# Sliding-window attention with a gated MLP: the values of batches 2 to 7 as 64x64 quarters, in one block with the next scores

## The chip, the cores and the metric

The kernel runs on one core of a Trainium2 chip. The metric is the device time of one execution in microseconds, the median of three runs. The engines are TensorE (matmuls; its weight loads are listed apart), VectorE, ScalarE, GpSimd, and the SP queue, which here only issues DMAs. Each works through its own instructions in the order in which the program lists them, and waits on semaphores for the others.

## The reference

```python
# attention: batch 8, heads 8, sequence 576, head_dim 64; window 128
scores = scale * np.matmul(q, k.transpose(0, 1, 3, 2))
rel = pos[:, None] - pos[None, :]
bias = slopes[:, None, None] * (-np.abs(rel))[None, :, :]
mask = (rel >= 0) & (rel < window)
scores = np.where(mask, scores + bias[None], -1000000000.0)
attn = softmax(scores)
x = np.matmul(attn, v)                 # (8, 8, 576, 64) -> 4608 tokens of 512
# MLP: d_model 512, d_ff 2048
h = x @ w_in
g = h * np.clip(h + 3.0, 0.0, 6.0) / 6.0
out = g @ w_out
```

A query sees itself and the 127 keys before it. With query blocks of 128 that is the block of its own (below the diagonal) and the one before (above the diagonal). With halves of 64 it is three key halves: its own, the one before, which lies wholly inside the window, and the one before that.

## The kernel before

The two stages run interleaved. Attention works on pairs of heads: `g` runs from 0 to 31, four pairs to a batch (`NP` = 4), and `e` is the head within the pair. The MLP works on nine tiles of 512 tokens. Its work is cut into units: an up (`moe_up`, 4 matmuls of 512 columns into an `hps` bank, then a relu on ScalarE and a product on VectorE that also frees the bank) and a quarter of a down (`moe_down`, 4 matmuls into `ops`). The order of ups and downs is a hand-written string (L564), and `fill(n)` issues the next n units; it stops early where an up needs tokens whose attention isn't marked `done`.

Batches 0 and 1 have code of their own (`first_batch`, `second_batch`). Batches 2 to 7 run in `segment` (L718), one turn for each `g` from 8 to 32. A turn issues the scores of `g`, then between units its exponentials and masks, and the values of `g - 1`. Every engine's order is the program's order (`manual_schedule`), so the place of a line in `segment` is its place in each queue.

- Scores (`scores`, L344): keys on the partitions of the result. From g = 9 on they are 20 matmuls on 64x64 quarters of the array (row half by head, column half by key half), up to 192 columns each, into the two tiles `sce` (two banks each, pool `ps_sc`). These two tiles are kept through all of the segment. At g = 8 `scores_whole` writes them with 128-row results, so that no part is left unwritten.
- Exponentials and masks: `exp_diag` and `exp_off` (L385, L410) turn `sce` into `pd` (own block), `po` (block before) and `p4buf` (the last 64 queries), bf16; the ALiBi bias is the activation's bias, by partition (`bias_d`, `bias_o`). GpSimd clears what lies outside the window by `affine_select` (L406, L415, L421).
- Values (`values`, L445): the probabilities are the weights, and the values with a column of ones (`vbuf`, 65 columns) are streamed. 18 matmuls on the whole array, in two parts of 10 and 8, each part into the one bank of `ps_av`. VectorE divides by the column of sums (L452, L453) into `avs`.
- `back` (L472): an SP transpose DMA brings `avs` to `xT`, the MLP's input; for g = 10 and 11 TensorE and ScalarE do.
- `stage_next` (L591): the loads of a later batch on the SP queue (`load_tokens`), GpSimd's casts into `tbuf` and `vbuf`, and the SP transposes from `tbuf` into `qTb` and `kTb` (`xbar`). There is one `tbuf`, so the cast of the keys waits until the queries' transpose has read it.
- `double` (L237): for g = 8 to 11, TensorE transposes of keys and queries of batches 2 and 3 through a PSUM bank.

PSUM pools before: `ps_sc` 2 tiles of two banks, `ps_av` 1 bank, `ps_h` 2 banks (ups, transposes), `ps_o` 1 bank (downs). A tile of a pool takes the bank of the tile allocated as many allocations earlier as the pool has buffers, and waits until that one's last reader is done.

## Time and profile before

| | |
|---|---|
| median of three runs | 322.15 us (321.69 to 322.75) |
| the profiled execution's span | 319.2 us |
| granted TensorE clock, mean | 0.999 |
| VectorE, ScalarE, GpSimd busy | 173.1, 195.7, 141.2 us |
| DMA | 51.90 MB, mean 163 GB/s |

The span runs from the first to the last instruction of the program in one profiled execution. Busy time is summed by engine. A timeline row gives the start, the length from the first start to the last end of merged instructions, engine, line, operation, result and operands, and a count. A group row of the page gives the busy time, the mean length of one, and the engine's idle time ahead of it. A row of one line's or tile's instructions gives the shortest, median and longest in ns, then the first and the last start in us. A matmul's length includes its way through the array, and the next starts before it ends. ScalarE's and VectorE's lengths also overlap a little with the next.

### The profile page before, as it was taken

Reading aid. Unit: us, or ns where it says so; the run is one execution under the profiler, and the core shown is the slowest. Engines: PE = TensorE matmul, PEld = TensorE weight load, DVE = VectorE, ACT = ScalarE, POOL = GpSimd, SP = SyncE. Lnnn points to the kernel's source line nnn. Section 1 sums busy time; section 2 is a strip of 40 time slices with the busy share of each in tenths; the row PEclk is TensorE's granted clock in tenths of the full one; section 3 lists DMA queues with packets and bytes.
Section 4 is the critical chain, followed back from the end, with each engine's and each line's share of the span. In section 5 each row is a group of like instructions: output and inputs, shape, how many; then the busy total and the mean of one; then the engine's idle time right before and its main releaser. Section 6 shows DMA issues by size and latency. Waiting matters only on the chain.

```text
span 319.2 us, 7124 instructions
## 1 busy us (share of the span) xinstructions
PE 310.1 (97%) x2775; PEld 164.9 (52%) x2775; DVE 173.1 (54%) x338; ACT 195.7 (61%) x334; POOL 141.2 (44%) x249
## 2 busy tenths in 40 slices
PE   7879999999999999999999999999999999999996
PEld 5565465455545454445677654444444444444443
DVE  6667675554355655655565556555656455455510
ACT  4748976877767776676676667666764344244401
POOL 8464493684496477266744673663331000000000
PEclk9999999999999999999999999999999999999999
DMA  7999999999999999998999999962212110000112
GB/s 281 199 323 225 256 260 195 249 231 194 215 252 157 239 208 211 205 222 194 207 205 211 209 190 196 225 93 68 38 39 88 53 36 33 33 33 35 66 56 75
DMA packets 131425, 51.90 MB, mean 163 GB/s; under 512 B 118976, under 2 KB 123328, under 8 KB 131392
## 3 DMA queue, kind: packets, MB, share of 16 engines
q1 hardware_dynamic: 126160, 45.36, 68.0%
q0 software_dynamic: 4224, 4.19, 8.2%
q10 hardware_dynamic: 1008, 1.90, 1.6%
q8 instruction: 21, 0.34, 0.5%
q14 instruction: 12, 0.10, 0.1%
HBM read 36.70 MB, written 9.44 MB: 145 GB/s over the span
## 4 chain that ended last, share of the span: by engine, by line
PE 86%; DMA 5%; ACT 4%; POOL 2%; DVE 2%; issue 1%; POOLq 0%
PE ops L552 38%; PE hps L502 36%; DMA w_in_sb<-in_moe_w_in_dram 3%; PE sce L365 3%; PE av L442 2%; PE av L434 2%; DMA ldbuf<-in_k_dram 2%; ACT r L521 2%; PE ops L533 1%; ACT kTb L245 1%; ACT gbuf L399 1%; PE tp L243 1%; DVE gbuf L522 0%; ACT gbuf L377 0%; PE tb L483 0%
## 5 line engine op out<-in xcount | busy, mean ns | idle before, releaser
L522 DVE SCALAR_TENSOR_TENSOR gbuf<-r,hps 128x512 bf16<-128x512 f32 x144 | 98.7, 688 | 101.0 <-ACT r L521 99.8
L521 ACT ACTIVATE r<-hps,bias 128x512 f32<-128x512 f32 x144 | 98.9, 689 | 86.8 <-PE hps L502 86.6
L502 PE MATMUL hps<-xT,w_in_sb 128*128 128x512 bf16 (+1 forms) x640 | 144.9, 358 | 0.6 <-ACT xT L489 0.3
L552 PE MATMUL ops<-w_out_sb,gbuf 128*128 128x512 bf16 x560 | 137.8, 379 | 0.0
L502 PEld LDWEIGHTS <-w_in_sb 128*128 128x128 bf16 x640 | 59.3, 98 | 55.0 <-issue 0.8
L552 PEld LDWEIGHTS <-gbuf 128*128 128x128 bf16 x560 | 51.9, 98 | 56.3
L415 POOL TENSOR_SCALAR_AFFINE_SELECT po<-po 128x512 bf16<-128x512 bf16 x48 | 30.3, 636 | 32.5 <-ACT po L413 32.4
L406 POOL TENSOR_SCALAR_AFFINE_SELECT pd<-pd 128x512 bf16<-128x512 bf16 x48 | 29.8, 634 | 33.5 <-ACT pd L389 33.5
L389 ACT ACTIVATE pd<-sce,bias_d 128x512 bf16<-128x512 f32 x48 | 31.7, 684 | 5.4 <-PE sce L373 2.7
L561 DVE COPY osb<-ops 128x512 f32<-128x512 f32 x33 | 22.7, 688 | 20.0 <-PE ops L552 17.5
L195 POOL CAST tbuf<-ldbuf 128x512 bf16<-128x512 f32 (+1 forms) x45 | 25.6, 614 | 16.8 <-issue 9.3
L413 ACT ACTIVATE po<-sce,bias_o 128x512 bf16<-128x512 f32 x48 | 33.0, 687 | 0.0
L453 DVE TENSOR_TENSOR avs<-av,rc 128x384 bf16<-128x384 f32 (+1 forms) x48 | 23.6, 491 | 1.6
L442 PEld LDWEIGHTS <-pd 128*128 128x128 bf16 x192 | 14.3, 97 | 8.3 <-issue 0.5
L434 PE MATMUL av<-vbuf,po 128*128 128x65 bf16 x192 | 18.0, 193 | 0.0
L442 PE MATMUL av<-vbuf,pd 128*128 128x65 bf16 x192 | 17.3, 193 | 0.3 <-ACT kTb L245 0.3
L434 PEld LDWEIGHTS <-po 128*128 128x128 bf16 x192 | 14.3, 98 | 2.9 <-DVE avs L453 0.5
L188 POOL CAST vbuf<-ldbuf 128x1024 bf16<-128x1024 f32 x14 | 14.2, 1043 | 3.5 <-DMA ldbuf<-in_v_dram 3.5
L418 ACT ACTIVATE p4buf<-sce,bias_d 128x64 bf16<-128x64 f32 x48 | 15.5, 323 | 0.0
L228 POOL CAST pr<-ldbuf 128x576 bf16<-128x576 f32 x20 | 12.9, 670 | 5.1 <-DMA ldbuf<-in_k_dram 3.1
L365 PE MATMUL sce<-qTb,kTb 64*64 64x192 bf16 (+1 forms) x368 | 11.9, 245 | 0.0
L365 PEld LDWEIGHTS <-kTb 64*64 64x64 bf16 x368 | 7.1, 106 | 8.6 <-issue 8.5
(104 smaller groups left out, 208.4 us busy)
## 6 DMA issues: line engine op xcount, KB each, us to landing
out_dram<-osb SPq DMA_DIRECT2D x33, 256.0 KB, 2.5
ldbuf<-in_v_dram SPq DMA_DIRECT2D x32, 256.0 KB, 5.2
ldbuf<-in_q_dram SPq DMA_DIRECT2D x20, 256.0 KB, 5.3
ldbuf<-in_k_dram SPq DMA_DIRECT2D x16, 256.0 KB, 4.4
ldbuf<-in_q_dram SPq DMA_DIRECT2D x12, 288.0 KB, 7.0
ldbuf<-in_k_dram SPq DMA_DIRECT2D x12, 288.0 KB, 6.3
w_in_sb<-in_moe_w_in_dram POOLq DMA_DIRECT2D x4, 512.0 KB, 9.2
w_out_sb<-in_moe_w_out_dram POOLq DMA_DIRECT2D x4, 512.0 KB, 10.3
```

What stands on the lines that cost most here:

```text
L195: nc.gpsimd.tensor_copy(out=tbuf[:m, :, j, :], in_=s[:m, j, :, :].rearrange("p (i e) d -> p i (e d)", e=2))
L365: nc.tensor.matmul(sce[e][lo:lo + 64, j, :, :].rearrange("p s c -> p (s c)")[:, ds(lo, n)], lhsT=kT[r, j, lo:lo + 64], rhs=qT[r, ds(128 * ...
L389: nc.scalar.activation(out=pd[:, e, :, :], in_=st["sce"][e][:, :, 0, :], func=ACT.Exp, bias=bias_d[:, h:h + 1], scale=scale)
L406: nc.gpsimd.affine_select(out=pd[:, e, :, :], in_=pd[:, e, :, :], pattern=[[0, 4], [1, 128]], channel_multiplier=-1, base=0, compare_op=AL ...
L413: nc.scalar.activation(out=po[:, e, :, :], in_=sc[:, :, 1, :], func=ACT.Exp, bias=bias_o[:, h:h + 1], scale=scale)
L415: nc.gpsimd.affine_select(out=po[:, e, :, :], in_=po[:, e, :, :], pattern=[[0, 4], [-1, 128]], channel_multiplier=1, base=-1, compare_op=A ...
L434: nc.tensor.matmul(out_av, lhsT=po[:, e, qt % 4 if full(g) else qt - 1, :], rhs=vb[:, qt - 1, h, :], start=True, stop=False)
L442: nc.tensor.matmul(out_av, lhsT=d, rhs=vb[:, qt, h, :], start=(qt == 0), stop=True)
L502: nc.tensor.matmul(hps[:, lo:hi], lhsT=w_in_sb[:, ks, ts(ms, 128)], rhs=xT[:, ks, ds(src, hi - lo)], start=(ks == 0), stop=(ks == n_ks - 1))
L521: nc.scalar.activation(out=r6, in_=hps, func=ACT.Relu, bias=bias3[:, 0:1], scale=1.0 / 6.0)
L522: nc.vector.scalar_tensor_tensor(out=gts[nt][:, ms, :], in0=r6, scalar=1.0, in1=hps, op0=ALU.min, op1=ALU.mult)
L552: nc.tensor.matmul(ops[nt, sub], lhsT=gts[nt][:, ms, ts(sub, 128)], rhs=w_out_sb[:, ms, :], start=(ms == 0), stop=(ms == n_ms - 1))
```

## The change

From batch 2 on, the scores and the values both go by quarters. A query half meets its own key half (`back` = 0), the one before (1) and the one before that (2). The scores of each `back` stand together in the score tile (`SLOT`, `COUNT`, `place`), so each is one activation for each head, six for a pair in all: 320, 256 and 256 columns. The mask for `back` = 0 and 2 is one `affine_select` for each partition half over both heads; `back` = 1 needs none. A quarter's result lies on the partition half given by the parity of the query half and by the head, so half of the value matmuls need the values on the other partition half: `vswap` is a copy of `vbuf` with its halves swapped, made by VectorE in four parts a batch.

In a turn, the values of `g - 1` now follow the scores of `g` at once; only the values of g = 8 come in the middle of turn 9, behind the four parts of `vswap` for batch 2. `back` is issued after the third unit. The exponentials come in the order 0, 2, 1, the last after the sixth unit. There are seven units in turns 9 to 16 and eight in the others; before, seven in turns 9 to 11 and 13 to 15, and eight in the others, as far as `fill` doesn't stop early. The pool `ps_av` goes, and `ps_h` has three banks: values take two of them at a time, and `double`, the warm-up and some of the first ups move to it. At g = 8 four matmuls of 512 columns write all of the score tiles ahead of the quarters. The biases by partition half (`bias_s`) are made ahead of the segment, and `bias_o` and `p4buf` go.

```diff
-    ps_av = ctx.enter_context(tc.tile_pool(name="ps_av", bufs=1, space=bass.MemoryType.PSUM))
-    ps_h = ctx.enter_context(tc.tile_pool(name="ps_h", bufs=2, space=bass.MemoryType.PSUM))
+    ps_h = ctx.enter_context(tc.tile_pool(name="ps_h", bufs=3, space=bass.MemoryType.PSUM))
...
+    def half_biases():
+        nc.vector.tensor_scalar(out=rel_f[64:128, :], in0=rel_f[64:128, :], scalar1=-64.0,
+                                scalar2=0.0, op0=ALU.add, op1=ALU.add)
+        for back in range(3):
+            for h in range(H):
+                nc.vector.tensor_scalar(out=bias_s[:, back, h:h + 1], in0=rel_f,
+                                        scalar1=-32.0 - 64.0 * back, scalar2=slopes[h],
+                                        op0=ALU.add, op1=ALU.mult)
...
+    COUNT = (5, 4, 4)
+    SLOT = (0, 9, 5)
+
+    def place(back, qh):
+        k, b = divmod(qh, 2)
+        return (k + 1) % NQ if back == 0 else k - (back + 1 - b) // 2
...
         if g == 2 * NP:
...
+            st["sc"] = [ps_sc.tile([128, 16 * 64], FP32, tag="sc", name="sc") for _ in range(2)]
+            for bank in range(2):
                 for e in range(2):
                     r = slice(e * D, (e + 1) * D)
...
+                    nc.tensor.matmul(st["sc"][e][:, ts(bank, 512)], lhsT=kT[r, 0:128],
+                                     rhs=qT[r, 0:512], start=True, stop=True)
+        for m in range(9):
+            both = m < 6
+            for back in (0, 1) if both else (0, 2, 1):
+                if m + back > 8:
+                    continue
+                qh = m + back
+                for e in range(2):
+                    r = slice(e * D, (e + 1) * D)
+                    c0 = 64 * (qh % 2 ^ e)
+                    at = SLOT[back] + place(back, qh)
+                    o = st["sc"][e][c0:c0 + 64, :].rearrange("p (j c) -> p j c", c=64)
+                    x = qT.rearrange("p (j c) -> p j c", c=64)
+                    if both and back == 0:
+                        o, x = o[:, at:at + 5:4, :], x[r, m:m + 3:2, :]
+                    else:
+                        o, x = o[:, at, :], x[r, qh, :]
+                    nc.tensor.matmul(o, lhsT=kT[r, ts(m, 64)], rhs=x, start=True, stop=True)
...
+    def exp_back(g, back, e):
+        h, p, n = 2 * (g % NP) + e, st[g, "p"][back], COUNT[back]
+        nc.scalar.activation(out=p[:, e, :, :].rearrange("p j c -> p (j c)"),
+                             in_=st["sc"][e][:, ds(64 * SLOT[back], 64 * n)], func=ACT.Exp,
+                             bias=bias_s[:, back, h:h + 1], scale=scale)
+        if e == 0 or back == 1:
+            return
+        for r in range(2):
+            half = p[ds(64 * r, 64), :, :, :].rearrange("p e j c -> p (e j) c")
+            sign, base = (1, 0) if back == 0 else (-1, -1)
+            nc.gpsimd.affine_select(out=half, in_=half, pattern=[[0, 2 * n], [sign, 64]],
+                                    channel_multiplier=-sign, base=base,
                                     compare_op=ALU.is_ge, fill=0.0)
...
+    def values(g):
+        b, hp = divmod(g, NP)
+        av = [ps_h.tile([128, NT], FP32, tag="h", name="av") for _ in range(2)]
+        steps = [[(qh, back) for qh in range(half, 9, 2) for back in range(3) if qh >= back]
+                 for half in range(2)]
+        steps[1].append((9, 0))
+        for i in range(len(steps[0])):
+            for half in range(2):
+                if i >= len(steps[half]):
+                    continue
+                qh, back = steps[half][i]
+                k, qh = qh // 2, min(qh, 7 + (half == 0))
+                at = place(back, qh)
+                for e in range(2):
+                    r = slice(64 * (half ^ e), 64 * (half ^ e) + 64)
+                    v = (vbuf if back % 2 == e else vswap)[b % 2]
+                    nc.tensor.matmul(av[e][ts(half, 64), ds(k * W, W)],
+                                     lhsT=st[g, "p"][back][r, e, at, :],
+                                     rhs=v[r, (qh - back) // 2, 2 * hp + e, :],
+                                     start=(back == 0),
+                                     stop=(back == min(2, qh) or k == 4 and half == 1))
+        avs = st[g, "avs"] = small.tile([128, NQ, 2, D], BF16, tag="avs", name="avs")
+        rc = small.tile([128, 2, NQ, 1], FP32, tag="rcw", name="rcw")
+        for e in range(2):
+            a = av[e][:, 0:NQ * W].rearrange("p (j c) -> p j c", j=NQ)
+            nc.vector.reciprocal(rc[:, e, :, :], a[:, :, D:W])
+            nc.vector.tensor_tensor(out=avs[:, :, e, :], in0=a[:, :, 0:D],
+                                    in1=rc[:, e, :, :].to_broadcast([128, NQ, D]), op=ALU.mult)
+
+    def swap_v(b, part):
+        lo, j0, j1 = ((0, 0, 3), (64, 0, 2), (0, 3, 5), (64, 2, 4))[part]
+        nc.vector.tensor_copy(
+            out=vswap[b % 2][ds(64 - lo, 64), j0:j1, :, :].rearrange("p j h c -> p (j h c)"),
+            in_=vbuf[b % 2][ds(lo, 64), j0:j1, :, :].rearrange("p j h c -> p (j h c)"))
...
+    UP_BANKS = {5: "o", 11: "o"}
...
+    FILLS = {g: 7 for g in range(9, 17)}
+
+    def segment(lo, hi):
         for g in range(lo, hi + 1):
+            b, hp = divmod(g, NP)
+            swaps = list(range(4)) if hp == 0 and b < B and g > lo else []
             if by_xbar(g - 2):
                 done[0] = g - 1
+            if lo < g < hi:
                 scores(g)
+            if g > lo + 1:
+                values(g - 1)
+            if g == 3 * NP:
+                cast_tokens(3, "v")
             turn = {2 * NP: (2, 1, "k"), 2 * NP + 1: (2, 1, "q"),
                     2 * NP + 2: (3, 0, "k"), 2 * NP + 3: (3, 1, "k")}.get(g)
             if turn:
+                double(*turn, 0, "h", A)
+            elif g < hi:
+                exp_back(g, 0, 0)
+            fill(1)
             if turn:
+                double(*turn, 1, *(("h", V) if turn[0] == 2 else ("h", A)))
+                exp_back(g, 0, 0)
+            fill(1)
             if g < hi:
+                exp_back(g, 0, 1)
+            fill(1)
+            if g > lo + 1:
+                back(g - 1)
+                if not by_xbar(g - 1):
+                    done[0] = g
             if g < hi:
+                exp_back(g, 2, 0)
+            for part in range(4):
+                if g == lo + 1:
+                    swap_v(2, part)
+            fill(1)
             if g < hi:
+                exp_back(g, 2, 1)
+            if swaps:
+                swap_v(b, swaps.pop(0))
+            if g == lo + 1:
+                values(g - 1)
+                back(g - 1)
+            fill(1)
             if g < hi:
+                exp_back(g, 1, 0)
+            if swaps:
+                swap_v(b, swaps.pop(0))
+            fill(1)
             if g < hi:
+                exp_back(g, 1, 1)
                 stage_next(g)
+            if swaps:
+                swap_v(b, swaps.pop(0))
             fill(1)
+            if swaps:
+                swap_v(b, swaps.pop(0))
+            fill(FILLS.get(g, 8) - 7)
```

125 lines of the change are left out of this document (14 added, 111 removed).

## The prediction

> **What bounds the kernel now.** I read the page first (busy shares and slices), then TensorE's waits, then its timeline around one pair of heads, then ScalarE, VectorE, GpSimd and the SP queue at the places the change touches.
>
> ```profile
> span 319.2 us, 7124 instructions
> PE 310.1 (97%) x2775; PEld 164.9 (52%) x2775; DVE 173.1 (54%) x338; ACT 195.7 (61%) x334; POOL 141.2 (44%) x249
> PE w L153 <- POOL ident masks.py:199: 1.4, 1, 1.4
> PE scd L297 <- DVE kTb L221: 1.1, 3, 0.4
> ```
>
> TensorE is busy for 97% of the span, and its list of waits, largest total first, begins with 1.4 us at the start and three that come to 1.1, none over 0.4. So the span is TensorE's stream of matmuls. What shortens that stream shortens the span, and every new wait of TensorE in batches 2 to 7 is paid in full. The other engines are far from full on average, so they matter only where TensorE must wait for one particular result.
>
> The stream around one pair of heads:
>
> ```profile
> 182.04 0.19 PE L434 MATMUL av<-vbuf,po 128*128 128x65 bf16 x1
> ...
> 182.28 1.04 PE L502 MATMUL hps<-xT,w_in_sb 128*128 128x256 bf16 x8
> 183.16 1.89 PE L552 MATMUL ops<-w_out_sb,gbuf 128*128 128x512 bf16 x8
> 184.98 0.52 PE L365 MATMUL sce<-qTb,kTb 64*64 64x192 bf16 x16
> 185.31 0.21 PE L373 MATMUL sce<-qTb,kTb 64*64 64x64 bf16 x4
> 185.46 1.90 PE L552 MATMUL ops<-w_out_sb,gbuf 128*128 128x512 bf16 x8
> 187.19 0.23 PE L442 MATMUL av<-vbuf,pd 128*128 128x65 bf16 x2
> ...
> 187.50 1.89 PE L502 MATMUL hps<-xT,w_in_sb 128*128 128x512 bf16 x8
> ```
>
> Eight matmuls of 512 columns take 187.19 - 185.46 = 1.73, so 0.216 each, 0.42 ns a column, and a unit of the second stage (four of them) 0.86. The eight at 183.16 end their stream at 184.89; the next unit begins at 185.46, so **one pair's scores cost 0.57**. Of that 0.09 passes before the first and about 0.10 after the last (its stream ends near 185.36): the price of going into 64x64 tiles and out. The stream between is 0.38. The two **values blocks cost 0.31 + 0.24 = 0.55**, with no gap on either side. Together 1.12 a pair.
>
> **The change, part by part.**
>
> *Does a quarter run beside three others?* Sixteen score matmuls start within 184.98 to about 185.28, 19 ns apart, though 192 columns take 80 ns: four run at once. For 64 columns with a weight load each, the nearest rows are the first batch's transposes, on two quarters:
>
> ```profile
> 10.33 0.76 PE L220 MATMUL tp<-ident,pr 64*64 64x64 bf16 x36
> L220 PE MATMUL tp<-ident,pr x144: 192/193/213, 5.3 to 13.7; 64*64 64x64 bf16 x144
> ```
>
> (0.76 - 0.19) / 35 = 16.2 ns a matmul, so 32 ns for a round of two, one on each quarter. I take 32 ns for a round of four, since `L365` shows four at once; the bounds are 27 (64 columns' stream) and 65 (four at 16.2).
>
> *Scores*: 36 matmuls for 20. In two key halves each quarter has one of 128 and one of 64 columns: 80 ns and two starts of 5, so 90; six key halves 0.27; in the last three the busier quarters have four of 64 columns, 0.13 more. About 0.39, as now. *Values*: 50 matmuls for 18, 13 rounds, 0.42. *The block*: 0.09 + 0.39 + 0.42 + 0.10 = 1.00 against 1.12. For g = 10 to 31 that is 22 x -0.12 = **-2.6**. Values alone, at g = 9 and 32, cost 0.61 against 0.55: +0.1. The first scores get four matmuls of 512 columns, two at a time (0.43), and a second change of tiling:
>
> ```profile
> 51.04 0.58 PE L336 MATMUL sce<-qTb,kTb 64*128 64x256 bf16 x8
> ...
> 51.59 1.04 PE L552 MATMUL ops<-w_out_sb,gbuf 128*128 128x512 bf16 x4
> ```
>
> 0.43 + 0.39 + 0.28 for entering twice and leaving = 1.1, against 0.55 and the 0.09 ahead of it: +0.45. TensorE's own sum: **-2.1**.
>
> [...]
>
> *Scores waiting for the last exponentials.* `sc` is rewritten by the next scores, so they wait for the last exponential of the pair before (`exp_back(g, 1, 1)`). It now comes after the sixth unit, leaving one unit before the scores for g = 9 to 16 and two after that; today's has two or three. Where that sixth unit is an up, its relu stands ahead on ScalarE:
>
> ```profile
> 192.06 1.03 PE L502 MATMUL hps<-xT,w_in_sb 128*128 128x512 bf16 x4
> 193.12 0.69 ACT L521 ACTIVATE r<-hps,bias 128x512 f32<-128x512 f32 x1 [1.04 <-PE hps L502]
> 193.71 0.68 ACT L389 ACTIVATE pd<-sce,bias_d 128x512 bf16<-128x512 f32 x1
> L418 ACT ACTIVATE p4buf<-sce,bias_d 128x64 bf16<-128x64 f32 x48 | 15.5, 323 | 0.0
> L389 ACT ACTIVATE pd<-sce,bias_d 128x512 bf16<-128x512 f32 x48 | 31.7, 684 | 5.4 <-PE sce L373 2.7 <-POOL tbuf L195 2.7
> ```
>
> The up's stream ends at 192.92, relu starts 0.2 later, the next exponential 0.59 after that; one of 256 columns takes 323 + 192 x 0.81 = 478 ns, between the two rows. So it ends 0.2 + 0.59 + 0.48 = 1.27 after the up, and scores after one unit and the change of tiling could start at 0.95: 0.32. With two units (1.73) nothing. By the list of units (L564) the sixth is an up and one unit follows at g = 9, 13, 14 and 15: 4 x 0.32 = **+1.3** (0 if relu finds ScalarE free sooner, 2.8 if one more exponential, 0.37 by the same slope, stands in between each time).
>
> *The shared ring.* The values now take two of three `ps_h` banks that the ups and the key and query transposes also take. The tile two allocations behind them gets the bank of `av[0]`, which VectorE frees:
>
> ```profile
> 65.43 0.19 DVE L452 RECIPROCAL rc<-av 128x6 f32<-128x6 f32 x1
> 65.66 0.56 DVE L453 TENSOR_TENSOR avs<-av,rc 128x384 bf16<-128x384 f32 x1
> ...
> 67.68 0.42 DVE L453 TENSOR_TENSOR avs<-av,rc 128x256 bf16<-128x256 f32 x1
> 53.32 0.44 PE L243 MATMUL tp<-ident,pr 128*128 128x128 bf16 x5
> 53.60 1.03 PE L552 MATMUL ops<-w_out_sb,gbuf 128*128 128x512 bf16 x4
> ```
>
> The last matmul's 0.19 less its 0.03 stream, 0.23 to the multiply, 0.49 for 320 columns (between 0.56 and 0.42): 0.92 with the hand-over. At g = 10 and 11 only five transposes (0.28) stand between values and that tile: 0.64 twice. At g = 15, 17, 21, 25, 29 one up does (0.86): 0.06 each. **+1.6** (0 to 3, if VectorE has a relu product ahead).
>
> *The swapped copy.* At g = 9 four copies, 1,560 and 3 x 1,040 columns, stand on VectorE ahead of `values(8)`, behind one up's product:
>
> ```profile
> 62.98 1.03 PE L502 MATMUL hps<-xT,w_in_sb 128*128 128x512 bf16 x4
> 64.83 0.69 DVE L522 SCALAR_TENSOR_TENSOR gbuf<-r,hps 128x512 bf16<-128x512 f32 x1 [0.93 <-ACT r L521]
> 2.87 1.76 DVE L135 TENSOR_SCALAR tab<-base 128x256 bf16<-128x256 bf16 x8
> L489 DVE COPY xT<-tb x1: 458/458/458, 50.0 to 50.0; 128x576 bf16<-128x576 bf16 x1
> L486 DVE COPY xT<-tb x1: 325/325/325, 23.2 to 23.2; 128x320 bf16<-128x320 bf16 x1
> L162 DVE TENSOR_SCALAR bias_d<-rel_f 128x1 f32<-128x1 f32 x8 | 0.6, 146 | 0.0
> ```
>
> `L489` and `L486` differ by 0.52 ns a column, from PSUM; `L135`, SBUF to SBUF as here, steps by 0.2 for 256 columns, which fits 0.26 a column and 0.13. So 4,680 columns take 1.7 (3.1 by the slower rows). They end at 65.5 + 1.7 = 67.2; the values block would start at 62.98 + 3 x 0.86 = 65.6 and can't end before about 67.4 rather than 66.1: **+1.3** (2.6 by the slower rows). The later copies, one batch ahead of use and beside down units, delay nothing that TensorE needs; without that cover each would add up to 0.5. The 25 small bias operations (0.6 / 8 = 0.07 each by `L162`, 1.9 together) stand on VectorE ahead of g = 8, under its first units on TensorE; uncovered they would cost those 1.9 once.
>
> [...]
>
> *Values that come earlier, masks that don't.* GpSimd's masks of a pair stand behind the cast of the next keys, which waits for the transpose of the queries:
>
> ```profile
> 133.43 2.84 POOL L195 CAST tbuf<-ldbuf 128x512 bf16<-128x512 f32 x5 [5.73 <-DMA qTb<-tbuf]
> 136.23 1.22 POOL L406 TENSOR_SCALAR_AFFINE_SELECT pd<-pd 128x512 bf16<-128x512 bf16 x2
> 137.41 1.22 POOL L415 TENSOR_SCALAR_AFFINE_SELECT po<-po 128x512 bf16<-128x512 bf16 x2
> 136.61 0.52 PE L365 MATMUL sce<-qTb,kTb 64*64 64x192 bf16 x16
> 138.82 0.23 PE L442 MATMUL av<-vbuf,pd 128*128 128x65 bf16 x2
> 120.00 1.23 SPq L476 DMA_TRANSPOSE xT<-avs  x1
> 121.28 4.44 SPq L112 DMA_DIRECT2D ldbuf<-in_k_dram  x5
> 125.83 3.75 SPq L200 DMA_TRANSPOSE qTb<-tbuf  x1
> ```
>
> The masks end at 138.6, and the values start at 138.82: 0.2 to spare. In the block they would start at 137.1, so 1.5 late, unless the SP queue reaches the key load and the transpose sooner. It stands back to back here, but `back` is now issued two units earlier and the loads of g = 12 stand further ahead of the next scores, so it should. The k load of the row at 121.28 has to start about 1.5 sooner against the scores. I take **+0.4** for one place, with 0 and 1.8 as bounds. ScalarE's exponentials fall from 2 x (684 + 684 + 323) to 2 x (530 + 2 x 478) ns a pair, 0.4 us less; the masks go from 2,176 to 2,304 columns, 2.7 us at these rows' pace. Both lie under the eight units of a pair, 6.9 us.
>
> *Sum*: -2.1 + 1.3 + 1.6 + 1.3 + 0.4 = +2.5 on the span of 319.2. The runs' median, 322.15, lies 2.9 above the span; I carry that over: **324.6**.
>
> **The rivals.**
> - *Faster.* ScalarE, VectorE and SP run ahead enough that no wait shows, and only the shorter stream is left: 322.15 - 2.1 = 320.0. For it: no such wait today. Against: the bank rings and the unit order leave the gaps above.
> - *No change.* About half of the waits come: -2.1 + 2.2, 322.2.
> - *Not four at once.* The quarters with 64 columns issue at 16.2 ns: 86 x 0.0162 + 0.19 = 1.58 a block, +0.58 for 23 blocks, 13.3 over the forecast, near 336 once the ring's waits are covered. For it: no row has four quarters with 64 columns. Against: `L365`. [...]
> - *GpSimd becomes the bound of the values.* The SP queue doesn't move up, and in four batches values wait 1.9 for masks: 7.6 - 0.4 over the forecast, 331.8. It decides once the key cast ends later than 2.7 before the block. For it: the 0.2 to spare and SP's unbroken chain.
>
> **How the numbers follow.** Forecast 0.42 (its own range 323.2 to 327.5), faster 0.19, no change 0.14, not four at once 0.09, GpSimd 0.16. The range 320.0 to 332.0 leaves out the slow-quarter case and half of the faster one. About 0.3% (1 us) can be told from no change: faster 0.19, same 0.14, slower 0.67.
>
> **What would show it.** The block from its first score matmul to the next unit: 0.9 if right, 1.4 if quarters don't overlap. TensorE's waits: on ScalarE's `p` before scores at g = 10, 14, 15, 16; on `avs` or `rc` before `tp2` and `hps`; on `vswap` once for over 1 us; on GpSimd's `p` near each key cast. If TensorE shows no waits past 60 us, the forecast is wrong on the fast side; if every block waits for masks, on the slow side.

## The result and the profile after

Four runs of the changed kernel have a median of 331.76 us (330.21 to 332.5); four of the kernel before, beside them, 322.44. The ratio is **1.0283, interval 1.0253 to 1.0313**: slower by 9.3 us, where 2.4 had been forecast. The profiled execution's span is 330.5 us against 319.2, so 11.3 longer; it is that of the longest of the four runs (332.5).

The head of the page of the kernel after:

```profile
span 330.5 us, 9436 instructions
PE 313.4 (95%) x3941; PEld 165.6 (50%) x3941; DVE 192.9 (58%) x379; ACT 186.4 (56%) x334; POOL 148.2 (45%) x223
```

TensorE's share falls from 97% to 95% in a longer span. So the time isn't work that was added to TensorE, but gaps. Its list of waits (total, times, longest, in us) names them:

```profile
PE av L451 <- DVE vswap L466: 7.0, 8, 1.7
...
PE hps L515 <- DVE avs L461: 0.9, 2, 0.5
```

Before, nothing stood above 1.4. Now the values wait for the swapped copy, eight times, 7.0 in all. A block is called by its turn below: the block of g = 12 holds the scores of g = 12 and the values of g = 11. TensorE's timeline around three of them, those of g = 9 (values alone), 12 and 14 (start, length in us; the values rows, which alternate between two tiles, are left out of the second and the third):

```profile
65.67 1.03 PE L515 MATMUL hps<-xT,w_in_sb 128*128 128x512 bf16 x4
66.62 0.21 PE L451 MATMUL av<-vbuf,p 64*64 64x65 bf16 x1
67.43 0.19 PE L451 MATMUL av<-vswap,p 64*64 64x65 bf16 x1 [0.59 <-DVE vswap L466]
...
68.35 0.19 PE L451 MATMUL av<-vswap,p 64*64 64x65 bf16 x1 [0.70 <-DVE vswap L466]
...
69.94 0.19 PE L451 MATMUL av<-vswap,p 64*64 64x65 bf16 x1 [1.24 <-DVE vswap L466]
...
70.34 1.89 PE L565 MATMUL ops<-w_out_sb,gbuf 128*128 128x512 bf16 x4
...
89.74 2.10 PE L565 MATMUL ops<-w_out_sb,gbuf 128*128 128x512 bf16 x9
91.78 0.54 PE L372 MATMUL sc<-qTb,kTb 64*64 64x128 bf16 x34
...
92.73 1.47 PE L565 MATMUL ops<-w_out_sb,gbuf 128*128 128x512 bf16 x6
...
107.37 1.89 PE L515 MATMUL hps<-xT,w_in_sb 128*128 128x512 bf16 x8
109.19 0.89 PE L372 MATMUL sc<-qTb,kTb 64*64 64x128 bf16 x36
...
110.46 1.04 PE L565 MATMUL ops<-w_out_sb,gbuf 128*128 128x512 bf16 x4
```

- The undisturbed block (g = 12): nine matmuls of 0.216 end at 89.74 + 1.94 = 91.68, the next unit begins at 92.73: 1.05, and other undisturbed ones take 1.02. The forecast was 1.00, before it was 1.12.
- g = 14: 107.37 + 8 x 0.216 = 109.10, the next unit begins at 110.46: 1.36. The scores stood 0.33 for the last exponential, as forecast (0.32).
- Values alone at turn 9: from the up's end (65.67 + 0.86 = 66.53) to the down at 70.34, 3.81, where an undisturbed one (in turn 32) takes 0.63. They run in drips, each released by a copy.

The same reckoning over all blocks accounts for the span. It measures each block from the end of the stream before it, so it finds 8.7 for the copies where the list of waits has 7.0: the list counts idle time only from the end of the last matmul's length, 0.19 after its start.

| place | us |
|---|---|
| values that wait for copies: g = 9 3.2, 13 2.7, 17 1.4, 21 and 25 0.7 each | 8.7 |
| low clock from 70 to 74 us (below) | 1.6 |
| scores that wait for the last exponential, four places | 1.3 |
| bank ring, g = 10 and 11 | 1.25 |
| first scores, g = 8: 1.14 for 0.64 | 0.5 |
| shorter blocks, 22 x -0.08 | -1.8 |
| sum, against 11.3 measured | 11.5 |

Why are the copies late? VectorE and GpSimd in turn 9:

```profile
65.79 0.69 DVE L535 SCALAR_TENSOR_TENSOR gbuf<-r,hps 128x512 bf16<-128x512 f32 x1 [0.93 <-ACT r L534]
66.51 3.37 DVE L466 COPY vswap<-vbuf 64x1560 bf16<-64x1560 bf16 x4
...
66.18 3.42 POOL L413 TENSOR_SCALAR_AFFINE_SELECT p<-p 64x640 bf16<-64x640 bf16 x4 [0.49 <-ACT p L405]
```

The four copies begin right behind the up's product, as in the forecast, but take 3.37 where it had 1.7, and they do so beside four masks on GpSimd that take 3.42 at the same time. The groups by shape show it for all 24 (busy, then mean ns of one), with the masks of both widths:

```profile
L466 DVE COPY vswap<-vbuf 64x1040 bf16<-64x1040 bf16 x18 | 12.6, 699 | 0.5
L466 DVE COPY vswap<-vbuf 64x1560 bf16<-64x1560 bf16 x6 | 4.7, 775 | 0.2
L413 POOL TENSOR_SCALAR_AFFINE_SELECT p<-p 64x640 bf16<-64x640 bf16 x48 | 37.5, 782 | 67.0 <-ACT p L405 56.5 <-issue 8.9
L413 POOL TENSOR_SCALAR_AFFINE_SELECT p<-p 64x512 bf16<-64x512 bf16 x48 | 32.7, 682 | 15.6 <-ACT p L405 12.0 <-POOL p L413 1.0
```

The last two copies, which start at 229.93 and 230.37, have no GpSimd instruction beside them, and take 426 ns each.

After that wait TensorE is granted about half of its clock. Stretches of 2 us (length; busy of TensorE, weight load, VectorE, ScalarE, GpSimd; granted clock; DMA share; GB/s):

```profile
68.00:70.00 2.00, 0.41 (x27) 0.30 (x30) 1.92 (x4) 0.15 (x1) 1.80 (x4) 1.00 1.26 218
70.00:72.00 2.00, 2.00 (x31) 0.86 (x31) 1.79 (x5) 0.00 (x0) 2.00 (x4) 0.54 1.08 222
72.00:74.00 2.00, 2.00 (x7) 0.80 (x6) 0.00 (x0) 0.15 (x1) 1.81 (x4) 0.61 0.43 96
```

Matmuls of 512 columns follow each other there by 0.427 in place of 0.216, seven or eight of them: 1.6 us. "Busy" reads 2.00 in both: only the clock column tells.

### The profile page after: what moved, and what is told of

Same layout as the page of the kernel before. It is cut to its first block, busy times and chain, and to the rows that moved or that the text cites. A ratio compares the mean times of both kernels' runs of the same rounds, so it can differ in the third digit from the quotient of the medians.

```text
span 330.5 us, 9436 instructions
## 1 busy us (share of the span) xinstructions
PE 313.4 (95%) x3941; PEld 165.6 (50%) x3941; DVE 192.9 (58%) x379; ACT 186.4 (56%) x334; POOL 148.2 (45%) x223
## 4 chain that ended last, share of the span: by engine, by line
PE 71%; DMA 12%; DVE 6%; SPq 4%; ACT 3%; issue 2%; POOL 1%; ACTq 0%; DVEq 0%; POOLq 0%
PE ops L565 32%; PE hps L515 31%; DMA w_out_sb<-in_moe_w_out_dram 5%; DVE vswap L466 5%; SPq L111 4%; DMA ldbuf<-in_k_dram 4%; PE av L451 3%; PE sc L372 3%; DMA ldbuf<-in_v_dram 3%; ACT r L534 2%; PE ops L546 1%; ACT p L405 1%; DVE gbuf L535 1%; POOL w_out_sb L173 1%; POOL gbuf L399 0%
## 5 line engine op out<-in xcount | busy, mean ns | idle before, releaser
L413 POOL TENSOR_SCALAR_AFFINE_SELECT p<-p 64x640 bf16<-64x640 bf16 (+1 forms) x96 | 70.2, 732 | 82.6 <-ACT p L405 68.5
L405 ACT ACTIVATE p<-sc,bias_s 128x320 bf16<-128x320 f32 (+1 forms) x144 | 65.2, 495 | 14.8 <-PE sc L372 14.1
L461 DVE TENSOR_TENSOR avs<-av,rcw 128x320 bf16<-128x320 f32 x48 | 23.6, 491 | 1.6
L451 PE MATMUL av<-vswap,p 64*64 64x65 bf16 x600 | 17.0, 196 | 7.0 <-DVE vswap L466 7.0
L451 PEld LDWEIGHTS <-p 64*64 64x64 bf16 x1200 | 14.5, 106 | 8.8 <-issue 8.7
L466 DVE COPY vswap<-vbuf 64x1040 bf16<-64x1040 bf16 (+1 forms) x24 | 17.2, 718 | 0.7
L451 PE MATMUL av<-vbuf,p 64*64 64x65 bf16 x600 | 16.6, 196 | 0.0
L372 PE MATMUL sc<-qTb,kTb 64*64 64x64 bf16 (+1 forms) x864 | 14.6, 202 | 0.4
L460 DVE RECIPROCAL rcw<-av 128x5 f32<-128x5 f32 x48 | 9.0, 188 | 5.4 <-PE av L451 5.4
L247 ACT COPY kTb<-tp 128x640 bf16<-128x640 bf16 (+1 forms) x7 | 5.2, 745 | 3.2 <-PE tp L245 3.2
```

What stands on the lines that cost most here:

```text
L372: nc.tensor.matmul(o, lhsT=kT[r, ts(m, 64)], rhs=x, start=True, stop=True)
L405: nc.scalar.activation(out=p[:, e, :, :].rearrange("p j c -> p (j c)"), in_=st["sc"][e][:, ds(64 * SLOT[back], 64 * n)], func=ACT.Exp, bia ...
L413: nc.gpsimd.affine_select(out=half, in_=half, pattern=[[0, 2 * n], [sign, 64]], channel_multiplier=-sign, base=base, compare_op=ALU.is_ge, ...
L451: nc.tensor.matmul(av[e][ts(half, 64), ds(k * W, W)], lhsT=st[g, "p"][back][r, e, at, :], rhs=v[r, (qh - back) // 2, 2 * hp + e, :], start ...
L461: nc.vector.tensor_tensor(out=avs[:, :, e, :], in0=a[:, :, 0:D], in1=rc[:, e, :, :].to_broadcast([128, NQ, D]), op=ALU.mult)
L466: nc.vector.tensor_copy(out=vswap[b % 2][ds(64 - lo, 64), j0:j1, :, :].rearrange("p j h c -> p (j h c)"), in_=vbuf[b % 2][ds(lo, 64), j0:j ...
```

## The experiments

Every time is a median of three rounds or more, beside the kernel before on the same chip; ratios are to that kernel. Its own median lay between 321.4 and 322.7 in these sessions, so a difference between two experiments can be about 1 us off; the more careful figure, by the ratios, stands beside it where it matters.

**1. Without the copies.**

```diff
-                    v = (vbuf if back % 2 == e else vswap)[b % 2]
+                    v = vbuf[b % 2]
...
-            swaps = list(range(4)) if hp == 0 and b < B and g > lo else []
+            swaps = []
...
-            for part in range(4):
-                if g == lo + 1:
-                    swap_v(2, part)
```

> Leaves out the swapped copy; half of the value matmuls read the values of the other partition half. Theory: the waits of the values for the copies (8.7 us of TensorE's gaps in six turns of the profiled execution) and the half clock that follows the longest of them (1.7 us) go, so 331.8 falls to 321 to 322.5, and no turn's block of scores and values is longer than 1.5 us. Rival, that the copies only stand where another wait would show (masks on GpSimd): under 4 us are won, and blocks of 2 us stay at g = 13 and 17.

327.05, ratio 1.0183 (1.013 to 1.0236). 4.7 less than with copies (3.2 by the ratios), not the 9 to 11 of the theory. The copies' waits are gone, but others stand in their place:

```profile
PE hps L515 <- DMA w_in_sb<-in_moe_w_in_dram: 1.6, 2, 0.9
PE av L451 <- POOL p L413: 1.6, 3, 0.6
...
PE hps L515 <- DVE avs L461: 1.0, 2, 0.5
```

The second row is new: the values of g = 22 wait for GpSimd's masks, and their block, that of g = 23, takes 3.51 instead of 1.05. Experiments 9 to 11 ask where that comes from. The first row lies before 30 us, far ahead of the copies; the scores of g = 9 start at 62.98 in this execution and at 62.06 in that of the changed kernel.

**2. Copies without masks beside them.** The masks of the turns with copies (9, 12, 16, 20, 24, 28) are left out.

```diff
-        if e == 0 or back == 1:
+        if e == 0 or back == 1 or g == 9 or (g > 9 and g % NP == 0):
             return
```

> Leaves out GpSimd's masks in turns 9, 12, 16, 20, 24 and 28, where the copies stand; the copies are as they were. Theory, that a copy and a GpSimd instruction exclude each other: the four copies of turn 9 take 1.8 us in place of 3.4 and the wait of values(8) falls from 3.2 to about 1.5; the mean of a copy falls from 718 ns to under 600; 3 to 5 us are won. Rival, that a copy across partition halves takes 0.72 us of itself: its mean stays above 690 ns and under 1.5 us are won.

328.44, ratio 1.0215 (1.0171 to 1.0259), 3.3 less than with all masks (2.2 by the ratios). The 24 copies of this kernel as one line's instructions (shortest, median, longest in ns):

```profile
L466 DVE COPY vswap<-vbuf x24: 425/426/889, 66.1 to 225.3; 64x1040 bf16<-64x1040 bf16 x18, 64x1560 bf16<-64x1560 bf16 x6
```

and as groups by shape:

```profile
L466 DVE COPY vswap<-vbuf 64x1040 bf16<-64x1040 bf16 x18 | 8.3, 462 | 0.5
L466 DVE COPY vswap<-vbuf 64x1560 bf16<-64x1560 bf16 x6 | 3.7, 614 | 0.2
```

A copy of 1,040 columns takes 426 ns wherever no GpSimd instruction lies beside it, against a mean of 699 before. In turn 9 GpSimd still casts, and the four copies take 2.56. The 17.3 us of copies become 12.0, so what holds a copy up is the GpSimd instruction beside it, and not that it crosses partition halves. The waits for `vswap` fall from 7.0 to 3.6; by blocks, 2.3, 1.8 and 0.7 of the 8.7 are left, at g = 9, 13 and 17. So the length of the copies accounts for some 3.9, and their place for the rest.

The masks hardly lengthen. Without any copy (experiment 1) they take:

```profile
L413 POOL TENSOR_SCALAR_AFFINE_SELECT p<-p 64x640 bf16<-64x640 bf16 x48 | 37.2, 775 | 55.9 <-ACT p L405 45.4 <-issue 9.0
L413 POOL TENSOR_SCALAR_AFFINE_SELECT p<-p 64x512 bf16<-64x512 bf16 x48 | 31.4, 654 | 15.7 <-ACT p L405 12.1 <-POOL p L413 1.0
```

That is 68.6 us in all against 70.2 in the changed kernel, while the copies there take 17.3 against 11.0 if each took its length alone. Nor do the two simply take turns: in turn 9 of the changed kernel four copies (1.84 alone) and four masks (4 x 0.775 = 3.10) end within 3.7 us of the first one's start.

**3. The last exponential one unit sooner.**

```diff
             if g < hi:
                 exp_back(g, 1, 0)
+                exp_back(g, 1, 1)
...
             if g < hi:
-                exp_back(g, 1, 1)
                 stage_next(g)
```

> Computes all. The last exponential of a pair is issued beside the one before it, one unit sooner. Theory, that scores at g = 10, 14, 15 and 16 wait 0.32 us each for it: 1.3 us are won, 330.5, and these blocks fall from 1.36 to 1.42 us to about 1.05. Rival, that the scores wait for something else (the values' bank, TensorE's own change of tiling): no block gets shorter and the time stays within 0.5 us.

331.07, ratio 1.0289 (1.0241 to 1.0337), 0.7 less than the changed kernel, not separable by the intervals. The place itself can be read in its timeline, g = 16:

```profile
122.24 1.03 PE L565 MATMUL ops<-w_out_sb,gbuf 128*128 128x512 bf16 x4
123.19 0.54 PE L372 MATMUL sc<-qTb,kTb 64*64 64x128 bf16 x34
...
124.12 1.04 PE L565 MATMUL ops<-w_out_sb,gbuf 128*128 128x512 bf16 x4
```

122.24 + 0.86 = 123.10 to 124.12 is 1.02, where the changed kernel had 1.36. The same holds at g = 15, and g = 10 falls from 1.42 to 1.11; g = 14 keeps 1.31, where the values now wait for a bank of the ring that an up's product frees. All blocks together fall by 1.1. The scores waits are what the forecast said.

**4. Exponential sooner, transposes ahead of the scores, no copies.**

```diff
+            if turn:
+                double(*turn, 0, "h", A)
+                double(*turn, 1, *(("h", V) if turn[0] == 2 else ("h", A)))
             if lo < g < hi:
                 scores(g)
```

> Leaves out the swapped copies (all values matmuls read the unswapped v), as the run without copies did (327.05), and moves two things: the last exponential of a pair is issued one unit sooner, and in turns 8 to 11 both parts of the key or query transposes come ahead of the scores, so that the up after the values block no longer stands two ring places behind av[0]. Theory (two separate waits, scores and ring): the run without copies shows four scores waits of 0.40, 0.43, 0.35 and 0.33 and two ring waits of 0.69 and 0.61 = 2.8 in all, so 324.2; blocks at g = 10, 13, 14, 15 near 1.05 and no wait of a TensorE hps on avs over 0.2. Rival (the waits only move, since ScalarE and VectorE then stand behind something else): 326 to 327.5, with new waits of the same size on other tiles.

327.57, ratio 1.0169 (1.0131 to 1.0208): no gain over experiment 1, the rival's number. Yet `hps` no longer waits for `avs`. The first of its waits:

```profile
PE av L451 <- POOL p L413: 2.5, 5, 0.6
```

The ring's 1.3 is won, and so are the scores waits. But about 0.28 is lost again inside the values at g = 10, 11 and 14, which now stand for their own bank of the ring: at 10 and 11 ScalarE must first copy the transposes out of it, at 14 VectorE must finish an up's product. (The list's next row, `ops` waiting 2.4 for `issue`, is no wait: where it stands, the first matmul of a down is missing from the trace.) What was won is spent on masks: 1.5 in the block of g = 15 and 2.6 in that of g = 23, and after the latter the clock falls again:

```profile
176.00:178.00 2.00, 2.00 (x43) 1.49 (x30) 1.27 (x4) 0.00 (x0) 0.00 (x0) 0.50 1.25 218
```

**5. Values apart from the scores, no copies.** The values stand behind the first unit again.

```diff
-            if g > lo + 1:
-                values(g - 1)
...
                 exp_back(g, 0, 0)
+            if g > lo + 1:
+                values(g - 1)
             fill(1)
```

> Leaves out the swapped copies (all values matmuls read the unswapped v), as the run without copies did (327.05), and takes the values out of the block with the scores: they stand behind the first unit of the turn, with a change of tiling of their own. Theory (the block saves one change of tiling): alone, scores take 0.60 and values 0.63 = 1.23 where the block takes 1.03, so 22 times 0.20 = 4.4 more, less the one wait for masks that the run without copies shows in a block (2.5) = 329.0. Rival (values that stand 0.9 later meet their masks, copies and banks later and cover more than the change of tiling costs): 326 or less.

334.79, ratio 1.0389 (1.0348 to 1.043), 7.7 above experiment 1 (6.6 by the ratios) and beyond the 329.0. Scores 0.60 and values 0.63 came out as reckoned, and the waits for masks are gone, but an up right behind the values now takes the bank of the up right ahead of them, whose product isn't done, and waits nearly 1 us for it, five times:

```profile
PE hps L515 <- DVE gbuf L535: 4.8, 5, 1.0
```

The values of turns 10 and 11 wait another 2.0 for the bank of the transposes ahead of them. So the one block is worth its change of tiling, 0.2 a pair, and also the time that the scores put between an up and the values, which take two places of the ring.

**6. Copies by DMA.** Two transfers a batch; casts of `v` a turn sooner; experiment 3's edit.

```diff
-        nc.vector.tensor_copy(
-            out=vswap[...
+        eng = nc.gpsimd if b == 2 else nc.scalar
+        eng.dma_start(out=vswap[...
```

> The swapped copy is made by DMA in place of VectorE (two transfers a batch, issued on GpSimd's queue for batch 2 and on ScalarE's queue after that), the casts of v stand a turn sooner so that the transfers have a turn to land, that of batch 2 before the first values turn, where GpSimd stands idle; the last exponential of a pair is issued one unit sooner. Theory (the copies cost time because they stand on VectorE beside GpSimd work and are late): without them on an engine no wait of values for vswap is left, nor the half clock after it, and the time comes to that of the run without copies less its scores waits, 327.05 - 1.5 = 325.5. Rival (DMA is 90% busy in this stretch, so the transfers push back the chain of loads and transposes and the masks come late): waits of values for GpSimd's masks over 4 in all, 328 or more.

350.42, ratio 1.086 (1.081 to 1.091), far above the theory's 325.5. The rival's "328 or more" came true, but not for its reason: the values wait 1.2 for masks and 14.4 for the transfers themselves. A second form with experiment 4's edit, later key casts and transfers issued at turn 4n:

```diff
+            if hp == 0 and 2 < b < B:
+                for part in range(2):
+                    swap_v(b, part)
...
+            if hp == 2 and 3 < b + 1 < B:
+                cast_tokens(b + 1, "k")
+                xbar(b + 1, "k")
```

> As the kernel with copies by DMA, and also: both parts of the transposes ahead of the scores in turns 8 to 11; the cast of the next keys moved behind the masks of its turn's pair, the cast of v behind the masks of the fourth pair; transfers of the copy behind the second unit of the turn before use. Theory (what is left beside the copies is ring and masks): 325.5 less ring 1.3 and masks 2.5 = 321.7, no wait for masks over 0.5. Rival (the later key cast makes the scores of the next batch late, or v lands late): 325 or more, with scores waiting for kTb or values for vswap.

346.53, ratio 1.0738 (1.0663 to 1.0813). Its values still wait 9.7 for the transfers, and its scores 2.2 for the keys. The waits of the first of the two:

```profile
PE av L451 <- DMA vswap<-vbuf: 14.4, 4, 7.3
PE hps L515 <- DMA xT<-avs: 6.3, 5, 2.5
```

and its transfers (KB, median us to landing):

```profile
vswap<-vbuf ACTq DMA_DIRECT2D x5, 325.0 KB, 5.9
...
vswap<-vbuf POOLq DMA_DIRECT2D x1, 325.0 KB, 9.6
```

The transfer of batch 2 is issued at 66 us, because the casts of `v` of batch 2 wait for its load until 61.7 and 64.0, and takes 9.6 to land. From 70 to 72 us the DMA share is 1.05 and from 72 to 74 it is 1.28, so the engines are full there, and this copy by DMA lands at about 75.6, where VectorE's four end at 69.9 in the changed kernel. Ups also wait for the transposes that bring `xT`; whether the transfers push those back, or the values that come late, isn't shown.

**7. Copies sooner.** First, `v` cast a turn sooner and the copies behind the first units of turn 4n; for batch 2 behind the first unit of turn 9, with values(8) two units later than in the change:

```diff
-    VCAST = {15: 4, 19: 5, 23: 6, 27: 7}
+    VCAST = {11: 3, 14: 4, 18: 5, 22: 6, 26: 7}
...
+            if swaps:
+                swap_v(b, swaps.pop(0))
             fill(1)
```

> Computes all. The values are cast one turn sooner and the four copies follow the first units of their turn instead of the last; values(8) comes after the seventh place in turn 9 instead of the fifth. Theory, that only the place of the copies is wrong: waits on the copies fall from 8.7 us to under 1.5, no half clock, 321 to 324 us. Rival, that VectorE has no room for them anywhere in these turns: the wait moves to the banks that VectorE frees, and under half of the 10 us is won.

332.83, ratio 1.0422 (1.037 to 1.0475), and unsteady: 326.7, 330.3, 331.4 and three from 334.3 to 335.7. The ratio fits the last three alone, so neither it nor the median says much here. In the profiled run (326.7) no wait for `vswap` is left; the largest new one is an up's for a bank that the late values(8) hold. Why the other five were slower isn't shown by that profile and stays open.

Then the same for the later batches, with batch 2 cast ahead of the segment, copied in turn 8, values(8) in the block of g = 9, and the edits of experiments 3 and 4:

```diff
+        cast_tokens(2, "v")
         half_biases()
         segment(2 * NP, G)
```

> All of the change, with the copies still on VectorE but sooner: v of batch 2 is cast before the first values turn, where GpSimd stands idle, its copies follow in that turn, and values(8) stand in the block with the scores of g = 9; later casts of v stand a turn sooner and their copies behind the first units of turn 4n; last exponential one unit sooner; both parts of the transposes ahead of the scores in turns 8 to 11. Theory (the copies cost time by being late, and the rest is the queue and the masks): no wait for vswap, and the time of the kernel without copies, 327 to 328. Rival (beside GpSimd the copies stretch its masks and casts wherever they stand): waits of values for masks over 5 in all, 330 or more.

334.26, ratio 1.0374 (1.0315 to 1.0433). The theory's 327 to 328 is missed; the rival's "330 or more" came true, but not for its reason, since the waits for masks are only 2.3 in all. GpSimd and VectorE in turn 8:

```profile
59.66 1.04 POOL L190 CAST vbuf<-ldbuf 128x1024 bf16<-128x1024 f32 x1 [9.78 <-DMA ldbuf<-in_v_dram]
...
63.06 0.94 DVE L466 COPY vswap<-vbuf 64x1560 bf16<-64x1560 bf16 x1 [3.45 <-POOL vbuf L190]
```

The cast stands 9.78 for the load, the copy 3.45 for the cast, and the relu products behind it on VectorE with it; a wait on the way to `vswap` became a wait of the ups for their banks, with a granted clock of 0.50 from 66 to 74. From the scores of g = 11 on, however, this kernel has no wait for a copy: 87.73 to 255.37, 167.6 us to the last values, against 169.5 (79.06 to 248.61) in experiment 4, which makes none.

**8. TensorE kept at work in turn 9.** Into columns of `av[0]` that nobody reads, in the changed kernel:

```diff
+        for _ in range(50 if g == 2 * NP else 0):
+            nc.tensor.matmul(av[0][:, 384:512], lhsT=ident, rhs=ident, start=True, stop=True)
```

> The changed kernel with 50 matmuls of 128 columns into unused columns of av[0] ahead of values(8), so that TensorE works while it waits for the swapped copy. Theory (the stretch at a granted clock of 0.54 to 0.61 from 70 to 74 us follows from TensorE standing idle in that wait): the clock stays near 1.0 there and the time falls by about 1.7, to 330.0. Rival (the clock falls for another reason, or the work added makes up for it): 331.5 or more, with the low clock still there.

330.83, ratio 1.025 (1.0206 to 1.0295), 0.9 less than the changed kernel, which the intervals don't separate. The clock is plain. The 50 matmuls in this kernel's timeline, and its stretches behind them:

```profile
66.01 2.95 PE L442 MATMUL av<-ident 128*128 128x128 bf16 x50
```

```profile
70.00:72.00 2.00, 2.00 (x11) 0.94 (x10) 1.26 (x5) 0.30 (x1) 2.00 (x4) 1.00 0.63 186
72.00:74.00 2.00, 1.89 (x93) 1.29 (x92) 1.36 (x3) 0.75 (x2) 1.33 (x3) 1.00 0.41 94
```

From the scores of g = 9 to those of g = 10 it takes 10.91 (61.54 to 72.45), the changed kernel 12.55 (62.06 to 74.61): 1.6 less, as reckoned. That the median fell by less has a reason in the runs: two of the changed kernel's four already had a mean clock of 0.999, and one of this kernel's four has 0.993. Over more runs it is clearer: of the twelve with these 50 matmuls (here and in experiment 11) eleven have 0.999 or 1.0, of the twelve of the changed kernel and of experiments 2 and 3 three.

**9. Experiment 4 with less on the SP queue.** The loads of `v` of batches 5 to 7 are left out.

```diff
         t = tokens(b, nm)
+        if nm == "v" and b > 4:
+            return
```

> The kernel without copies and with the doubles ahead (327.57), which also leaves out the loads of v for batches 5 to 7 from memory (their casts run on what the buffer holds). Theory (from about 95 to 190 us the SP queue of loads and transposes is never idle, so it paces the turns: the masks of a pair stand behind the key cast, the key cast behind the transpose of the queries, that behind the loads): each load left out takes 4.3 to 5.8 off the queue of its batch; the wait for masks at g = 22 (2.6) and the stretch at granted clock 0.50 after it (about 1.4) go, those before turn 17 stay: 327.57 - 4.0 = 323.6. Rival (GpSimd itself is too slow for its masks and casts): the wait at g = 22 stays and the time is 327 or more.

323.49, ratio 1.0036 (1.0003 to 1.0069): the theory's number, 4.1 under experiment 4 (4.3 by the ratios). The SP queue around the queries' transpose, and GpSimd's cast of the keys and masks behind it, first of experiment 4, then of this one:

```profile
157.06 5.76 SPq L111 DMA_DIRECT2D ldbuf<-in_k_dram  x5
162.94 3.76 SPq L202 DMA_TRANSPOSE qTb<-tbuf  x1
...
169.88 2.83 POOL L197 CAST tbuf<-ldbuf 128x512 bf16<-128x512 f32 x5 [5.94 <-issue]
172.67 3.06 POOL L413 TENSOR_SCALAR_AFFINE_SELECT p<-p 64x640 bf16<-64x640 bf16 x4
```

```profile
155.41 4.36 SPq L113 DMA_DIRECT2D ldbuf<-in_k_dram  x5
160.22 4.10 SPq L204 DMA_TRANSPOSE qTb<-tbuf  x1
...
166.51 2.84 POOL L199 CAST tbuf<-ldbuf 128x512 bf16<-128x512 f32 x5 [1.27 <-issue]
170.16 3.06 POOL L415 TENSOR_SCALAR_AFFINE_SELECT p<-p 64x640 bf16<-64x640 bf16 x4 [0.81 <-ACT p L407]
```

In experiment 4 the masks begin the moment the key cast ends (172.67), so the cast holds them; here they wait for ScalarE, and the block of g = 23 takes 1.13 in place of 3.67, with no half clock behind it (the profiled run's mean clock is 1.0, experiment 4's 0.995). The wait of the values of g = 14, ahead of the first load left out, stays.

**10. The kernel before with the same loads left out**, by the same edit.

> The kernel before, leaving out the same loads of v for batches 5 to 7 (their casts run on what the buffer holds). Theory (TensorE's stream is the bound before, the queue only stands at its edge): 321.5 to 322.5, no change. Rival (the queue already paces the kernel before): 319 or less.

322.49, ratio 0.9989 (0.9961 to 1.0017): no change. Before, TensorE's stream is the bound, and the queue only stands just behind it.

**11. All copies made, none late from batch 3 on.** From batch 3 on the copies of the second kernel of experiment 7, in turn 9 the changed kernel's order with the work of experiment 8, and the edits of experiments 3 and 4.

```diff
-    VCAST = {15: 4, 19: 5, 23: 6, 27: 7}
+    VCAST = {11: 3, 14: 4, 18: 5, 22: 6, 26: 7}
...
             fill(1)
...
+            if swaps and g > lo:
+                swap_v(b, swaps.pop(0))
             fill(1)
```

> All of the change with its copies: those of batch 2 where the change has them, with the 50 matmuls ahead of values(8) that keep TensorE at work; from batch 3 on v is cast a turn sooner and the copies stand behind the first units of turn 4n; last exponential one unit sooner; both parts of the transposes ahead of the scores in turns 8 to 11. Theory (copies that stand a turn ahead of use cost nothing): up to the scores of g = 11 as with the busy wait (81.1) less ring and one scores wait (1.6), then 167.6 to the last values and 76.4 after them, as in the run with copies sooner: a span near 323.5 and a time of 325.5. Rival (copies beside masks cost time wherever they stand): 328 or more, with waits for masks over 5 in all.

327.22, ratio 1.0167 (1.011 to 1.0224): the best version with the change, 1.7 over the theory's 325.5 and under the rival's 328. Its 24 copies:

```profile
L468 DVE COPY vswap<-vbuf x24: 424/767/932, 66.2 to 222.9; 64x1040 bf16<-64x1040 bf16 x18, 64x1560 bf16<-64x1560 bf16 x6
```

They are as slow as ever (median 767), nobody is listed as waiting for one from batch 3 on, and the time equals that of experiments 1 and 4, which make no copy. In turn 9 the copies are as late as before, and the 50 matmuls (66.25 to 69.21) fill the time. The same with experiment 9's edit:

> As the run before in this list, and it leaves out the loads of v for batches 5 to 7 from memory (their casts run on what the buffer holds). Theory (what is then left of the difference is the queue of loads and transposes, through the masks): 3 to 4 less than with the loads, near 322, within 1 of the kernel before although all copies are made. Rival (the copies, not the queue, make the masks late): no more than 1 less.

326.95, ratio 1.0139 (1.008 to 1.0199): no gain, the rival's number. Its one mask wait, that of the values of g = 18, stays (the block takes 2.50, 2.66 with the loads). The first load left out would be issued in turn 17, behind the transpose on which that wait hangs, so this run doesn't tell queue from copies.

## Why the prediction was right and wrong

The sign and the range were right; the size was off by a factor of four, and the failed step is **the swapped copy**: +1.3, with the sentence that the later copies, "one batch ahead of use and beside down units, delay nothing that TensorE needs". In the profiled execution the copies of turn 9 cost 3.2 in place of 1.3, the later ones 5.5 in place of nothing, and the low clock 1.6.

- *The copies are not a batch ahead.* They stand behind units four to seven of turn 4n, and their values are at the head of turn 4n + 1; in turns 12 and 16 no unit stands between the last copy and the block. In place of the one wait for `vswap` that the prediction looked for there are eight. Where the copies are moved three units and a cast up (experiment 11), the waits of the later batches go.
- *Their length.* 1.7 for four was right for copies alone (3 x 0.426 + 0.559 = 1.84) and wrong beside masks (3.37). The 0.26 ns a column in it was an estimate fitted to one row; the copies alone show (559 - 426) / 520 = 0.26. Experiment 2 bears out half of its theory: a copy of 1,040 columns takes 426 ns alone, against 699 in the mean in the changed kernel. That a copy and a GpSimd instruction exclude each other for their whole length isn't so here, since the masks keep nearly their length (782 and 682 ns against 775 and 654), and four copies and four masks end within 3.7 us. The 3.1 "by the slower rows" was nearer, for another reason.
- *What they cost.* 8.7 of waits and 1.6 of clock in the profiled execution. But taking them away brings 4.7 (3.2 by the ratios), not 10.
- *The other terms of the sum held.* Block 1.02 to 1.05 for 1.00; four quarters of 64 columns do run at once (the 86 matmuls of the block of g = 12 start within 0.83 us, where one every 16.2 ns would make 1.4), so that rival is out. Scores waits 4 x 0.33 for 4 x 0.32, at the four places named. Ring 0.64 and 0.61 for 0.64 twice. First scores +0.5 for +0.45. All were confirmed in the trace; but experiments 3 and 4, which take the scores and ring waits out, win no time that the intervals separate.
- *GpSimd as the bound* was a rival with 0.16, and wasn't what happened: in the changed kernel no values wait for masks, so the +0.4 for one such place measured nothing either. It is what happens next. With the copies' waits out, values catch up with the masks, whose key cast stands behind the queries' transpose on a queue that, in experiment 4, isn't idle from 95 to 185 us. From batch 5 on experiment 9 shows that (4.1 us for three loads); experiment 10 shows that before, it cost nothing. What makes the masks of g = 14 late in experiment 4, and those of g = 18 in experiment 11, stays open.
- *The sum as a method.* Every term was priced against TensorE's stream, as if nothing lay just below it. With 0.2 us to spare for the masks, which the prediction quoted, a wait that is removed isn't won: the next one takes it.

## What to carry to other kernels

Before a copy is called ahead of its use, count the units between its place in the queue and the first reader, not the batches. Price a VectorE copy from SBUF to SBUF by what GpSimd does in the same microseconds (here 426 ns alone, up to 886 beside masks). And where two chains run within a few tenths of each other, as TensorE and the loads do here, expect a removed wait to come back on the other one, and test by lightening that one.

## What the runs showed of the hardware

- A bf16 copy from SBUF to SBUF on VectorE takes 426 ns for 1,040 columns alone (experiment 2, and the last two of the changed kernel) and, in the changed kernel, up to 886 ns with GpSimd's masks beside it. The masks lengthen far less: their means are 782 and 682 ns for 640 and 512 columns in the changed kernel, 775 and 654 where there are no copies (experiment 1).
- After waits of 3.2 us in turn 9 TensorE was granted 0.54 and 0.61 of its clock in two stretches of 2 us, though it was busy throughout; at half rate (0.427 us for 512 columns in place of 0.216) that is 1.84 + 1.56 = 3.4 us. After a wait of 2.6 (experiment 4, g = 23) it was granted 0.50 from 176 to 178 us, and experiment 2, with a wait of 2.3 at g = 9, has a mean clock of 0.994 or 0.995 in all four of its runs. After waits of 2.5 (experiment 1, g = 23) and 2.7 (changed kernel, g = 13), also with a few matmuls in between, the clock read 1.00 in the profiled executions (174 to 181 us and 98 to 106 us). Work put into the wait kept it at 1.00 in the profiled execution of experiment 8. So standing idle set it off in turn 9, but these lengths alone don't say when it does, and no run here shows what else decides.
- A transfer of 325 KB within SBUF took 5.9 us to land (9.6 for the first) in experiment 6, where the DMA share was 1.05 from 70 to 72 us and 1.28 from 72 to 74.
